# A Conformer block with its convolution moved into one attention loop over both batches

## The chip, the cores and the metric

The kernel runs on one core of a Trainium2 chip. The metric is the device time of one execution in microseconds (us); the median of the runs shown is compared.

## What is computed

A macaron Conformer block on x of shape (2, 4000, 512) in bf16, width D = 512, feed-forward width F = 2048, kernel width K = 3:

```python
h = _layernorm(x);  x1 = x + 0.5 * (_silu(h @ w_ff1_a) @ w_ff1_b)
h = _layernorm(x1)
q, k, v = h @ w_q, h @ w_k, h @ w_v
p = _softmax(einsum('btd,bsd->bts', q, k) * D ** -0.5)
x2 = x1 + einsum('bts,bsd->btd', p, v) @ w_o
h = _layernorm(x2) @ w_pw1
h = h[..., :D] * _sigmoid(h[..., D:])
hp = pad(h, one row of zeros before and after each batch)
dc = sum over i of hp[:, i:i + T, :] * dw[i]
dc = (dc - mean) / sqrt(var + 1e-5)      # mean and var over all 8000 rows
x3 = x2 + _silu(dc) @ w_pw2
x4 = x3 + 0.5 * (_silu(_layernorm(x3) @ w_ff2_a) @ w_ff2_b)
return _layernorm(x4)
```

The statistics of dc need every row of both batches before the first row of x3 can be formed.

## The kernel before

The 8000 rows are 16 chunks of 500 (eight per batch), each four tiles of 125 rows. x stays in SBUF for the whole kernel and is updated in place by `residual` (VectorE). Every matmul product is laid out so that TensorE streams 500 or 512 columns. There are eight PSUM banks: four "score" banks handed out in a ring by `sbank` (tile `s` in the profile), four "Y" banks (tile `y`) for sums that run over many steps.

The order of work is written out by hand. Each loop step emits its matmuls, then `hook` and `tick`; `after(n, fn)` puts `fn` n ticks ahead, `lags` holds the second half of earlier steps, and `pop` emits it. Each engine runs its instructions in the order emitted, waiting on semaphores that `Sync` derives from buffers read and written; a transfer's waits stand in the queue of the engine that issues it.

- `ln_job`: LayerNorm of a chunk: four `bn_stats` and aggregates on VectorE, a power on GpSimd, four normalisations (L492 on VectorE or, for the conv stage, L439 on ScalarE), and four DMA transposes issued on SyncE (L447) that give the feature-major copy `lnT` (or `hT` for keys).
- `ff_chunk`: for each of 16 slices of F, four matmuls, Silu on ScalarE, and four steps later the four matmuls of the second product into the Y banks.
- Keys: `wq wk` and `wv wo` are folded into `M` and `Wvo` at the start, so the normalised rows themselves are keys and values: `h` (row-major, 32 tiles of 128 with three rows of zeros set by `zero_keys`, L869) and `hT`. One batch's keys fill the region named `keys`.
- `attention(b)`: for eight query chunks, 32 key tiles each: four score matmuls, Exp on ScalarE, a running f32 sum on VectorE (L635), and four key tiles later the four value matmuls. `q_group` makes the next chunk's queries at key tiles 14 to 20. `finish_queries` copies the four Y banks out (ScalarE and VectorE, L661), splits the running sum in two bf16 halves (L665, L666), and puts `sums` two ticks and four `project` steps four to seven ticks later.
- `conv`: for 16 chunks and four feature blocks jj, the two halves of pw1 (eight matmuls), Sigmoid on ScalarE, the product on VectorE into `G` (L710), one-column halo copies on GpSimd, and one chunk later `depthwise`: three matmuls with diagonal tap matrices (`taps`), a copy to `dcv` on ScalarE and `bn_stats` on VectorE. `dcv` of all 16 chunks fills the `keys` region, free after attention.
- After the statistics: `swish` (ScalarE) and `pw2` (16 matmuls) of four chunks ahead, then FF2 over 16 chunks with `swish` and `pw2` of later chunks in its hook, and `out_job` for the last LayerNorm and the store.

`program` runs: FF1 of batch 0, attention of batch 0, FF1 of batch 1, attention of batch 1, conv, FF2. The weights of FF1 are loaded on ScalarE's queue at the start; FF2's first weights (`load_wa`) on SyncE's during the second attention, its second ones (`load_wb`) after conv. A second copy of the program, for scores too large for an unshifted exponential, is compiled behind a flag (`any_score`) and does not run on these inputs.

Of the kernel before, what the change touches and what calls it, by code (L numbers as in the profile page):

```python
# [13 lines left out]
TILE = 125  # L14
# [38 lines left out]
class Sync:  # L53
# [3 lines left out]
    def __init__(self, nc, n_dma_sems=40):  # L57
# [131 lines left out]
class Region:  # L189
# [13 lines left out]
    def buf(self, name, off, nbytes):  # L203

        assert off + nbytes <= self.nbytes, name
        b = Buf(name)
        for lo, hi, a in self.spans:
            if lo < off + nbytes and off < hi:
                b.alias.append(a)
                a.alias.append(b)  # L210
        self.spans.append((off, off + nbytes, b))
        return b


class Conformer:
    LN_SLOTS = 4
    NP = 8
    NG = 3
# [11 lines left out]
    def memory(self):  # L230
# [16 lines left out]
        self.dcv = [[A.view(t * 4096 + cc * 1024, CHUNK) for cc in range(DC)] for t in range(NCK)]  # L247
        self.b_dcv = [[A.buf("dcv", t * 4096 + cc * 1024, 1000) for cc in range(DC)]
# [11 lines left out]
        self.b_Wa = [Buf("Wa%d" % k) for k in range(self.NWA)]  # L260
# [46 lines left out]
        self.Wp1 = C.view(oM, DC * 2 * D).rearrange("p (c f) -> p c f", c=DC)  # L307
        self.b_Wp1 = C.buf("Wp1", oM, 8192)
# [4 lines left out]
        gof = [16384 + k * 4096 for k in range(self.NG)]  # L313
# [4 lines left out]
        o = 16384 + self.NG * 4096  # L318
        self.sig = [W.view(o + s * 1024, CHUNK) for s in range(2)]
        self.b_sig = [W.buf("sig", o + s * 1024, 1000) for s in range(2)]  # L320
        o += 2048
        self.bst = W.view(o, DC * NCK * 6, F32).rearrange("p (c t s) -> p c t s", c=DC, t=NCK)
        self.b_bst = [W.buf("bst", o + cc * NCK * 24, NCK * 24) for cc in range(DC)]
        self.dwd = [C.view(oACC + i * 256, 128) for i in range(DC * KW)]
        self.b_dwd = [C.buf("dwd", oACC + i * 256, 256) for i in range(DC * KW)]
# [6 lines left out]
        assert off[0] == 47104  # L332

# [55 lines left out]
        self.b_out = [Buf("out%d" % c) for c in range(NCK)]  # L389

# [50 lines left out]
    def load(self, dst, src, writes, eng="SP"):  # L441
        k = self.S.dsems[self.nxt("ld", 12)]
        return self.S.dma(eng, k, lambda e: e.dma_start(dst, src), writes=writes)

    def transpose(self, dst, src, reads, writes):
        k = self.S.dsems[12 + self.nxt("tr", 16)]
        return self.S.dma("SP", k, lambda e: e.dma_start_transpose(dst, src), reads=reads, writes=writes)  # L447

# [51 lines left out]
    def ln_job(self, c, at, kind, eng="DVE", gap=1):  # L500
# [3 lines left out]
        def tile(ti):  # L504
            if kind == "key":
                k = c % TCB
                tok, b_tok = self.h[k * TPC + ti], self.b_h[k * TPC + ti]
                feat, b_feat = self.hT[k][:, ti], self.b_hT[k][ti]
            else:
                tok, b_tok = self.ltm[ti], self.b_ltm[ti]  # L510
                feat, b_feat = self.lnT[c % 2][:, ti], self.b_lnT[c % 2][ti]
            self.ln_norm(c, sl, ti, tok[0:TILE, :], b_tok, eng)
            self.transpose(feat, tok, [b_tok], [b_feat])
# [98 lines left out]
    def attention(self, b, old, hook, done):  # L612
        S = self.S
        LAG = 4
        for qc in range(TCB):
            s = qc % 2
            if self.any_score:
                self.row_max(qc)
            for kt in range(TB):
# [19 lines left out]
                def values(kt=kt, p=p, qc=qc):  # L639
# [8 lines left out]
                if qc == 0 and kt < LAG:  # L648
                    self.pop({0: old // 2, 1: old - old // 2}.get(kt, 0))
                else:  # L650
# [43 lines left out]
    def conv(self, old, hook):  # L694
        S = self.S
        for t in range(NCK):
            gs, gp = t % self.NG, (t - 1) % self.NG
            for jj in range(DC):
                halves = []
                for cb in (DC + jj, jj):  # L700
                    ps, b_ps = self.sbank()
                    out = ps[:, 0:CHUNK].rearrange("p (t k) -> p t k", t=TPC)
                    for cc in range(DC):
                        self.mm(out, self.Wp1[:, cc, cb * 128:(cb + 1) * 128], self.lnT[t % 2][:, :, cc, 0:TILE],
                                cc == 0, cc == DC - 1, [self.b_Wp1] + self.b_lnT[t % 2], b_ps)
                    halves.append((ps, b_ps))
                (pb, b_pb), (pa, b_pa) = halves
                ss = self.nxt("sig", 2)
                self.act(self.sig[ss], pb[:, 0:CHUNK], AF.Sigmoid, [b_pb], [self.b_sig[ss]])
                S.op("DVE", lambda e, pa=pa, ss=ss, jj=jj, gs=gs: e.tensor_tensor(  # L710
                    out=self.G[gs][:, jj, 1:1 + CHUNK], in0=pa[:, 0:CHUNK], in1=self.sig[ss], op=ALU.mult),
                    reads=[b_pa, self.b_sig[ss]],
                    writes=[self.b_G[gs][jj], self.b_Gl[gs][jj], self.b_Gr[gs][jj]])
                self.halo(t, jj)
                if t >= 1:
                    self.lags.append(lambda t=t, jj=jj: self.depthwise(t - 1, jj))
                if t == NCK - 1:
                    self.lags.append(lambda t=t, jj=jj: self.depthwise(t, jj))
                if t == 0:
                    self.pop({0: old // 2, 1: old - old // 2}.get(jj, 0))  # L720
                elif t > 1 or jj > 1:
                    self.pop(1)
                hook(t, jj)
                self.tick()

    def halo(self, t, jj):

        S = self.S
        gs, gp = t % self.NG, (t - 1) % self.NG
# [11 lines left out]
    def depthwise(self, t, cc):  # L741
        S, gs = self.S, t % self.NG
# [20 lines left out]
    def taps(self):  # L763
# [6 lines left out]
        S.op("DVE", lambda e: e.tensor_copy(self.dwT, ps[:, 0:DC * KW].rearrange("p (c k) -> p c k", c=DC)),  # L770
             reads=[b_ps], writes=[self.b_dwT])
        for i in range(DC * KW):
            S.op("DVE", lambda e, i=i: e.tensor_scalar(
                self.dwd[i], self.ident, self.dwT[:, i // KW, i % KW:i % KW + 1], None, ALU.mult),
                reads=[self.b_ident, self.b_dwT], writes=[self.b_dwd[i]])
# [91 lines left out]
    def zero_keys(self):  # L867
        for k in range(TB):
# [3 lines left out]
    def program(self, any_score):  # L872
# [21 lines left out]
        self.zero_keys()  # L894
# [7 lines left out]
        def ff1(c, old):  # L902
            def hook(f):
                if f == 0 and c + 2 < NCK:
                    self.load_x(c + 2)
                if f == 1 and c + 1 < NCK and (c + 1) % TCB:
                    self.ln_job(c + 1, 1, "in")
                if c == 0 and f == 8:
                    weights()
                if c == NCK - 1 and f == 1:  # L910
                    pass

            self.ff_chunk(c, old, hook, lambda: self.ln_job(c, 5, "key"))

        def ff2_weights():
            for k in range(self.NWA):
# [118 lines left out]
```

## Time and profile before

| | us |
|---|---|
| median of 3 runs | 2277.57 (2275.61 to 2277.70) |
| profiled execution | 2278.08 |
| its span, first to last instruction | 2274.3 |

| engine | busy us | share |
|---|---|---|
| TensorE (PE), matmuls | 2131.4 | 94% |
| VectorE (DVE) | 989.3 | 43% |
| ScalarE (ACT) | 804.1 | 35% |
| GpSimd (POOL) | 122.0 | 5% |

The mean granted TensorE clock is 0.974. In the profile's lines the first numbers of a timeline row are its start and duration in us, "x" counts instructions merged in it, and "[t <-who]" is the engine's idle time just before it and what ended it. L435 is the helper through which every matmul goes, L439 that of every ScalarE instruction, L443 and L447 those of loads and transposes. SPq and ACTq are DMA issues in those engines' queues. Tile names are those of memory regions: `work`, `wff`, `keys`, `xt`.

### The profile page before, as it was taken

What the parts mean: (1) busy time and instruction counts of PE and PEld (TensorE: products, weight loads), DVE (VectorE), ACT (ScalarE), POOL (GpSimd) and SP (SyncE); (2) the same over time, 40 slices, a digit from 0 to 9 for tenths busy, and PEclk for the clock granted to TensorE, in tenths of its full rate; (3) what the DMA queues carried; (4) which work ended last, traced back from release to release, by engine and by line L of the source; (5) the groups of instructions that cost most, each with busy time, mean ns of one, the idle gap of its engine ahead of it and who ended that gap; (6) DMA issues with size and microseconds to landing.
All of it is one profiled execution on the core that took longest, in us unless ns stands there. A gap on an engine that the chain in (4) does not pass through costs nothing.

```text
span 2274.3 us, 24679 instructions
## 1 busy us (share of the span) xinstructions
PE 2131.4 (94%) x9828; PEld 1063.6 (47%) x9830; DVE 989.3 (43%) x2013; ACT 804.1 (35%) x1362; POOL 122.0 (5%) x283
## 2 busy tenths in 40 slices
PE   3999999999999999999999999977677999999996
PEld 1555544444444555544444444432233555555553
DVE  4333344444445344334444444554445543444432
ACT  1433333333333333333333333333445433333332
POOL 3000000000000000000000000011111000000000
PEclk9999999999999999999999999988778999999998
DMA  7122000000000022220000000011112111111110
GB/s 166 36 60 58 23 10 1 1 1 1 1 1 13 25 56 56 37 56 1 1 1 1 1 1 4 26 29 37 35 30 56 24 33 37 37 32 34 35 41 27
DMA packets 176144, 63.69 MB, mean 28 GB/s; under 512 B 146194, under 2 KB 175509, under 8 KB 176021
## 3 DMA queue, kind: packets, MB, share of 16 engines
q1 hardware_dynamic: 169620, 57.84, 11.4%
q10 hardware_dynamic: 6400, 4.20, 0.7%
q8 instruction: 79, 1.29, 0.2%
q14 instruction: 45, 0.36, 0.0%
HBM read 18.68 MB, written 8.19 MB: 12 GB/s over the span
## 4 chain that ended last, share of the span: by engine, by line
PE 87%; DVE 6%; ACT 3%; issue 2%; POOL 1%; DMA 1%; SPq 0%; POOLq 0%; DVEq 0%; ACTq 0%
PE s L435 49%; PE y L435 38%; ACT work L439 2%; DVE work L469 2%; POOL work L479 1%; DVE work L661 1%; DVE work L492 1%; DVE wff L749 1%; DVE work L666 0%; DMA xt<-in_x_dram 0%; DVE work L635 0%; ACT keys L439 0%; ACT wff L439 0%; DVE work L475 0%; DVE work L665 0%
## 5 line engine op out<-in xcount | busy, mean ns | idle before, releaser
L439 ACT ACTIVATE work<-s 128x500 bf16<-128x500 f32 (+1 forms) x1068 | 626.5, 587 | 1270.2 <-PE s L435 1265.1
L435 PE MATMUL y<-wff,work 128*125 128x512 bf16 (+1 forms) x2240 | 574.2, 384 | 0.0
L435 PE MATMUL s<-work,wff 128*128 128x500 bf16 x2048 | 511.2, 378 | 35.7 <-DMA work<-work 35.7
L635 DVE TENSOR_TENSOR work<-work 128x500 f32<-128x500 f32 x496 | 336.9, 679 | 474.1 <-ACT work L439 473.2
L435 PE MATMUL y<-work,keys 128*128 128x500 bf16 x2048 | 519.0, 374 | 2.0
L435 PE MATMUL s<-work,keys 128*128 128x500 bf16 x2048 | 517.4, 375 | 0.3
L435 PEld LDWEIGHTS y<-wff,work 128*125 128x125 bf16 (+1 forms) x2240 | 301.2, 134 | 204.2 <-issue 11.2
L435 PE MATMUL s<-work 128*128 128x500 bf16 (+3 forms) x1158 | 296.6, 393 | 87.6 <-ACT wff L439 64.1
L435 PEld LDWEIGHTS s<-work,wff 128*128 128x128 bf16 x2048 | 200.9, 98 | 258.0 <-issue 39.2
L435 PEld LDWEIGHTS y<-work,keys 128*128 128x128 bf16 x2048 | 198.1, 97 | 244.5 <-DVE work L661 15.3
L435 PEld LDWEIGHTS s<-work,keys 128*128 128x128 bf16 x2048 | 199.2, 98 | 229.0 <-DVE work L572 1.2
L530 DVE SCALAR_TENSOR_TENSOR xt<-y,xt 125x512 bf16<-125x512 f32 x128 | 79.5, 684 | 384.9 <-PE y L435 384.9
L435 PEld LDWEIGHTS s<-work 128*125 128x125 bf16 (+2 forms) x1158 | 137.9, 128 | 224.6 <-ACT wff L439 75.7
L469 DVE BATCH_NORM_STATS2 work<-xt 125x6 f32<-125x512 bf16 x320 | 200.3, 680 | 7.5 <-DMA xt<-in_x_dram 7.5
L479 POOL TENSOR_TENSOR work<-work 125x4 f32<-125x4 f32 x80 | 80.7, 1008 | 1928.5 <-DVE work L477 1928.5
L530 DVE SCALAR_TENSOR_TENSOR xt<-s,xt 125x512 bf16<-125x512 f32 x64 | 43.8, 691 | 132.5 <-PE s L435 132.5
L710 DVE TENSOR_TENSOR wff<-s,wff 128x500 bf16<-128x500 f32 x64 | 43.4, 677 | 113.4 <-ACT wff L439 77.4
L492 DVE TENSOR_SCALAR work<-xt,work 125x512 bf16<-125x512 bf16 x196 | 85.5, 482 | 11.0 <-POOL work L479 10.7
L439 ACT ACTIVATE work<-xt,work 125x512 bf16<-125x512 bf16 x60 | 43.9, 801 | 79.2 <-POOL work L486 79.2
L435 PE MATMUL s<-keys,work 128*128 128x500 bf16 x256 | 63.9, 376 | 0.0
L530 DVE SCALAR_TENSOR_TENSOR xt<-s,work,xt 125x512 bf16<-125x512 f32 x64 | 48.1, 751 | 29.3 <-PE s L435 29.3
L749 DVE BATCH_NORM_STATS2 wff<-keys 128x6 f32<-128x500 bf16 x64 | 43.2, 675 | 25.0 <-ACT keys L439 24.7
(46 smaller groups left out, 372.3 us busy)
## 6 DMA issues: line engine op xcount, KB each, us to landing
xt<-in_x_dram SPq DMA_DIRECT2D x15, 500.0 KB
out_dram<-work SPq DMA_DIRECT2D x15, 500.0 KB
work<-work SPq DMA_TRANSPOSE x192, 2.5
wff<-in_w_ff_a_dram ACTq DMA_DIRECT2D x8, 256.0 KB
wff<-in_w_ff_b_dram ACTq DMA_DIRECT2D x8, 256.0 KB
wff<-in_w_ff_a_dram SPq DMA_DIRECT2D x8, 256.0 KB
wff<-in_w_ff_b_dram SPq DMA_DIRECT2D x4, 512.0 KB
keys<-keys SPq DMA_TRANSPOSE x64, 2.4
```

Source lines behind the costliest of these rows:

```text
L435: self.S.op("PE", lambda e: e.matmul(out, lhsT, rhs, start=start, stop=stop), reads=reads, writes=[bank], inc=stop if inc is None else inc)
L439: return self.S.op("ACT", lambda e: e.activation(out, in_, func, **kw), reads=reads, writes=writes)
L469: self.S.op("DVE", lambda e: e.bn_stats(self.st[sl][:, ti, :], self.XT[g]), reads=[self.bx[g]], writes=[self.b_st[sl][ti]])
L479: S.op("POOL", lambda e: e.tensor_tensor(out=self.rs[sl], in0=self.va[sl], in1=self.neghalf[0:TILE, :], op=ALU.pow), reads=[self.b_va[sl], ...
L492: self.S.op("DVE", lambda e: e.tensor_scalar(out, self.XT[g], self.mv[sl][:, ti, 0:1], self.rs[sl][:, ti:ti + 1], ALU.subtract, ALU.mult), ...
L530: self.S.op("DVE", lambda e: e.scalar_tensor_tensor(out=self.XT[g], in0=ps, scalar=scalar, in1=self.XT[g], op0=ALU.mult, op1=ALU.add), rea ...
L635: S.op("DVE", lambda e, p=p: e.tensor_tensor(out=self.acc[s], in0=self.acc[s], in1=self.P[p], op=ALU.add), reads=[self.b_P[p], self.b_acc[ ...
L661: S.op("DVE", lambda e, dc=dc: e.tensor_copy(self.OT[:, dc, :], self.Yb[dc][:, 0:CHUNK]), reads=[self.b_Y[dc]], writes=[self.b_OT[dc]])
L710: S.op("DVE", lambda e, pa=pa, ss=ss, jj=jj, gs=gs: e.tensor_tensor(out=self.G[gs][:, jj, 1:1 + CHUNK], in0=pa[:, 0:CHUNK], in1=self.sig[s ...
L749: S.op("DVE", lambda e: e.bn_stats(self.bst[:, cc, t, :], self.dcv[t][cc]), reads=[self.b_dcv[t][cc]], writes=[self.b_bst[cc]])
```

## The change

FF1 runs over all 16 chunks first. Batch 0's keys go to `h` and `hT` as before; batch 1's normalised rows (`"key2"`) go through a staging tile `h2` to an HBM tensor `keys2`. One attention loop then runs over all 16 query chunks g; `second_keys` loads and transposes batch 1's key tiles from HBM as batch 0's tiles are used up, from key tile 6 of g = 7 to key tile 5 of g = 8. The LayerNorm of a finished query chunk starts with its last `project`, its normalisations on VectorE. Its pw1 work is issued in four `pair`s: at key tiles 22 and 27 of the next query chunk and 1 and 6 of the one after. A pair is `conv_b` (four matmuls, Tanh) and one tick later `conv_a` (four matmuls, the gate from sigmoid(b) = (1 + tanh(b / 2)) / 2, with the factor of a half put into the taps). Chunks 0 to 12 take their taps on VectorE (`taps_beside`: three operations, the middle results in f32, then `bn_stats`) and store the result to the HBM tensor `dcvd`; `fetch_conv` brings it back into `dcv` during the last query chunk and after it. Chunks 13 to 15 keep `depthwise` on TensorE, with pw1 of chunks 14 and 15 behind the loop. Wp1 now lies over FF1's first weights, so all FF2 weights are loaded after the last pw1, on ScalarE's queue: five pieces before the last two `depthwise`, the rest behind them and behind a Silu of one element. `zero_keys` is split over the FF1 chunks 0 to 7; the taps are prepared during FF1.

```diff
+        self.Wp1 = W.view(0, DC * 2 * D).rearrange("p (c f) -> p c f", c=DC)
+        self.b_Wp1 = W.buf("Wp1", 0, 8192)
...
+        self.stage = [W.view(8192 + cc * 1024, CHUNK) for cc in range(DC)]
+        self.b_stage = [W.buf("stage", 8192 + cc * 1024, 1000) for cc in range(DC)]
+        self.tmp = W.view(12288, CHUNK, F32)
+        self.b_tmp = W.buf("tmp", 12288, 2000)
+        self.bst = W.view(14848, DC * NCK * 6, F32).rearrange("p (c t s) -> p c t s", c=DC, t=NCK)
+        self.b_bst = [W.buf("bst", 14848 + cc * NCK * 24, NCK * 24) for cc in range(DC)]
+        gof = [16384, 20480]
...
+        self.h2 = [C.view(oQ1 + j * 1024, D) for j in range(TPC)]
+        self.b_h2 = [C.buf("h2", oQ1 + j * 1024, 1024) for j in range(TPC)]
...
+        self.keys2 = nc.dram_tensor("keys2", [TB * 128, D], BF16, kind="Internal").ap()
...
+        self.dcvd = nc.dram_tensor("dcvd", [self.NBESIDE, 128, DC * CHUNK], BF16, kind="Internal").ap()
...
+            if kind == "key2":
+                self.ln_norm(c, sl, ti, self.h2[ti][0:TILE, :], self.b_h2[ti], eng)
+                if ti == TPC - 1:
+                    k = c % TCB
+                    dst = self.keys2[k * 512:(k + 1) * 512, :].rearrange("(t p) d -> p t d", p=128)
+                    self.store(dst, self.h2c, self.b_h2, [self.b_keys2[k]])
+                return
...
-        for qc in range(TCB):
+        for g in range(NCK):
+            b, qc = divmod(g, TCB)
...
-                if qc + 1 < TCB and kt in (14, 16, 18, 20):
-                    self.q_group(b, qc + 1, (kt - 14) // 2)
-                hook(qc, kt)
+                if g + 1 < NCK and kt in (14, 16, 18, 20) and not (self.any_score and g + 1 == TCB):
+                    self.q_group((g + 1) // TCB, (g + 1) % TCB, (kt - 14) // 2)
+                if not self.any_score:
+                    if g == TCB - 1 and kt >= 6:
+                        self.second_keys(kt - 6)
+                    if g == TCB and kt < 6:
+                        self.second_keys(TB - 6 + kt)
+                hook(g, kt)
                 self.tick()
+    def second_keys(self, kt):
+        kc, kj = divmod(kt, TPC)
+        src = self.keys2[kt * 128:(kt + 1) * 128, :]
+        self.load(self.h[kt], src, [self.b_h[kt]], reads=[self.b_keys2[kc]])
+        self.transpose(self.hT[kc][:, kj], src, [self.b_keys2[kc]], [self.b_hT[kc][kj]])
...
-        self.after(2, sums)
+        last = b * TCB + qc == NCK - 1
+        self.after(1 if last else 2, sums)
         for ti in range(TPC):
-            self.after(4 + ti, lambda ti=ti: project(ti))
...
+            self.after((2 if last else 4) + ti, lambda ti=ti: project(ti))
...
+    def conv_b(self, t, jj):
+        ps, b_ps = self.pw1(t, DC + jj)
+        k = jj % 2
+        self.act(self.th[k], ps[:, 0:CHUNK], AF.Tanh, [b_ps], [self.b_th[k]], scale=0.5)
+    def conv_a(self, t, jj):
+        ps, b_ps = self.pw1(t, jj)
+        k, gs = jj % 2, t % 2
+        self.S.op("DVE", lambda e: e.scalar_tensor_tensor(
+            out=self.G[gs][:, jj, 1:1 + CHUNK], in0=self.th[k], scalar=1.0, in1=ps[:, 0:CHUNK],
+            op0=ALU.add, op1=ALU.mult),
+            reads=[b_ps, self.b_th[k]],
+            writes=[self.b_G[gs][jj], self.b_Gl[gs][jj], self.b_Gr[gs][jj]])
+        self.halo(t, jj)
+    def pw1(self, t, cb):
+        s = 1 if t == NCK - 1 else 0
+        ps, b_ps = self.sbank()
+        out = ps[:, 0:CHUNK].rearrange("p (t k) -> p t k", t=TPC)
+        for cc in range(DC):
+            self.mm(out, self.Wp1[:, cc, cb * 128:(cb + 1) * 128], self.lnT[s][:, :, cc, 0:TILE],
+                    cc == 0, cc == DC - 1, [self.b_Wp1] + self.b_lnT[s], b_ps)
+        return ps, b_ps
+    def taps_beside(self, t, cc):
+        S, g = self.S, self.G[t % 2][:, cc, :]
+        rd = [self.b_G[t % 2][cc], self.b_Gl[t % 2][cc], self.b_Gr[t % 2][cc], self.b_dwT]
+        w = [self.dwT[:, cc, k:k + 1] for k in range(KW)]
+        tmp, b_tmp = self.tmp, self.b_tmp
+        S.op("DVE", lambda e: e.tensor_scalar(tmp, g[:, 0:CHUNK], w[0], None, ALU.mult), reads=rd, writes=[b_tmp])
+        S.op("DVE", lambda e: e.scalar_tensor_tensor(
+            out=tmp, in0=g[:, 1:1 + CHUNK], scalar=w[1], in1=tmp, op0=ALU.mult, op1=ALU.add),
+            reads=rd + [b_tmp], writes=[b_tmp])
+        def rest():
+            S.op("DVE", lambda e: e.scalar_tensor_tensor(
+                out=self.stage[cc], in0=g[:, 2:2 + CHUNK], scalar=w[2], in1=tmp, op0=ALU.mult, op1=ALU.add),
+                reads=rd + [b_tmp], writes=[self.b_stage[cc]])
+            S.op("DVE", lambda e: e.bn_stats(self.bst[:, cc, t, :], self.stage[cc]),
+                 reads=[self.b_stage[cc]], writes=[self.b_bst[cc]])
+            self.store(self.dcvd[t][:, cc * CHUNK:(cc + 1) * CHUNK], self.stage[cc],
+                       [self.b_stage[cc]], [self.b_dcvd[t][cc]])
+        self.after(1, rest)
+    def fetch_conv(self, t):
+        self.load(self.dcv4[t], self.dcvd[t].rearrange("p (c k) -> p c k", c=DC), self.b_dcv[t],
+                  reads=self.b_dcvd[t])
...
-        self.zero_keys()
...
-                if f == 1 and c + 1 < NCK and (c + 1) % TCB:
+                if f == 1 and c + 1 < NCK:
                     self.ln_job(c + 1, 1, "in")
+                if c < TCB and f == 6:
+                    self.zero_keys(c)
                 if c == 0 and f == 8:
                     weights()
...
+                if c == 1 and f == 1:
+                    self.load(self.dwr, i["dw"], [self.b_dwr])
+                    self.after(6, self.taps)
+                if c == TCB - 1 and f < TPC:
+                    self.S.op("POOL", lambda e: e.memset(self.h2[f], 0.0), writes=[self.b_h2[f]])
+            self.ff_chunk(c, old, hook, lambda: self.ln_job(c, 5, "key" if c < TCB else "key2"))
...
+        for c in range(NCK):
+            ff1(c, old)
             old = len(self.lags)
...
+        for dc in range(DC):
+            self.q_group(0, 0, dc)
+        def pair(t, jj):
+            self.conv_b(t, jj)
+            self.after(1, lambda: self.conv_a(t, jj))
+            if t > 0:
+                self.after(3, lambda: self.taps_beside(t - 1, jj))
+        tail = NCK - 2
+        def att_hook(g, kt):
+            if g == 0 and kt == 8:
+                self.load(self.Wp1, i["w_pw1"].rearrange("(c p) f -> p c f", p=128), [self.b_Wp1])
+            if 0 <= g - 1 < tail and kt in (22, 27):
+                pair(g - 1, (22, 27).index(kt))
+            if 0 <= g - 2 < tail and kt in (1, 6):
+                pair(g - 2, 2 + (1, 6).index(kt))
+            if g == NCK - 1:
+                if 8 <= kt < 20 and not any_score:
+                    self.tap_matrix(kt - 8)
+                if kt >= 8 and kt % 4 == 0:
+                    for t in (kt // 4 - 2, TCB + kt // 4 - 2):
+                        if t < self.NBESIDE:
+                            self.fetch_conv(t)
+        self.attention(old, att_hook, lambda c: self.ln_job(
+            c, 1, "in", gap=1 if c < NCK - 1 else 0, slot=1 if c == NCK - 1 else 0))
+        if any_score:
+            for k in range(DC * KW):
+                self.tap_matrix(k)
+        steps = []
+        for jj in range(DC):
+            steps += [lambda jj=jj: self.conv_b(tail, jj), lambda jj=jj: self.conv_a(tail, jj)]
+        self.pop(3)
+        steps.pop(0)()
+        steps.pop(0)()
+        self.pop(1)
+        self.tick()
+        steps.pop(0)()
+        for _ in range(5):
+            self.tick()
+        while steps:
+            steps.pop(0)()
+            self.tick()
+        for cc in range(DC):
+            self.depthwise(tail - 1, cc)
+            self.tick()
+        for t in range(6, TCB):
+            self.fetch_conv(t)
+        while self.later:
+            self.tick()
+        self.load(self.Wp2, i["w_pw2"].rearrange("(c p) f -> p c f", p=128), [self.b_Wp2])
+        for jj in range(DC):
+            self.conv_b(tail + 1, jj)
+            if jj:
+                self.depthwise(tail, jj - 1)
+            self.conv_a(tail + 1, jj)
+            if jj:
+                self.depthwise(tail + 1, jj - 1)
+        clear = (14848 - 12288) // (F // self.NWA * 2)
+        for k in range(clear):
+            self.load_wa(i["w_ff2_a"], k, "ACT")
+        self.depthwise(tail, DC - 1)
+        self.depthwise(tail + 1, DC - 1)
+        self.act(self.nr1, self.onef, AF.Silu, [self.b_onef], [self.b_nr1])
+        for k in range(clear, self.NWA):
+            self.load_wa(i["w_ff2_a"], k, "ACT")
         for k in range(4):
-            self.load_wb(i["w_ff2_b"], 4 * k, 4 * k + 4)
+            self.load_wb(i["w_ff2_b"], 4 * k, 4 * k + 4, "ACT")
```

More of the change, by code (lines that the diff above doesn't have):

```diff
@@ L203, in buf, with bufs @@
     def buf(self, name, off, nbytes):
-        assert off + nbytes <= self.nbytes, name
+        return self.bufs(name, [(off, nbytes)])
+    def bufs(self, name, pieces):
         b = Buf(name)
[L207 to L211, printed above, removed]
+        for off, nbytes in pieces:
+            assert off + nbytes <= self.nbytes, name
+            for lo, hi, a in self.spans:
+                if lo < off + nbytes and off < hi and a not in b.alias:
+                    b.alias.append(a)
+                    a.alias.append(b)
+        self.spans += [(off, off + nbytes, b) for off, nbytes in pieces]
         return b
@@ L940, in conv_hook @@
-        def conv_hook(t, jj):
-            if t == 0 and jj == 2:
-                self.load(self.dwr, i["dw"], [self.b_dwr])
-                self.after(2, self.taps)
-            if t == 4 and jj == 0:
-                self.load(self.Wp2, i["w_pw2"].rearrange("(c p) f -> p c f", p=128), [self.b_Wp2])
-            if jj == 0 and t + 1 < NCK:
-                self.ln_job(t + 1, 0, "in", "ACT", gap=0)
-        self.conv(old, conv_hook)
-        self.drain()
+                if c == 1 and f == 1:
+                    self.load(self.dwr, i["dw"], [self.b_dwr])
+                    self.after(6, self.taps)
```

129 lines of the change are left out of this document (43 added, 86 removed).

## Prediction

> **What bounds the kernel now.** I read the page's busy shares and slices first, then busy time by stage, then what TensorE waited for, then the timeline at the three places where it idles.
>
> ```profile
> span 2274.3 us, 24679 instructions
> PE   3999999999999999999999999977677999999996
> PEclk9999999999999999999999999988778999999998
> 274.00:765.00 491.00, 485.88 (x2316) 227.17 (x2314) 226.51 (x360) 166.37 (x285) 2.01 (x2) 1.00 0.02 4
> 1484.00:1758.00 274.00, 197.66 (x728) 80.75 (x726) 132.12 (x287) 116.43 (x194) 40.05 (x173) 0.81 0.17 39
> PE s L435 <- ACT wff L439: 64.1, 14, 4.7
> PE s L435 <- DMA work<-work: 35.7, 1, 35.7
> PE s L435 <- DVE work L666: 7.8, 16, 0.5
> ```
>
> Lines 2 and 3 are tenths in 40 slices; the two rows with a colon give, for one stage, its length and the busy time of PE, PEld, DVE, ACT, POOL, then granted clock, DMA share and GB/s. TensorE is the bound everywhere but in two places: the first slice and the conv stage. The first attention keeps it busy 485.88 of 491 us at clock 1.00, DVE and ACT under half. The conv stage has 197.66 of 274 us at clock 0.81, and those busy microseconds are stretched. The last rows are TensorE's waits (total, times, longest): 14 waits on ACT in the conv stage, one start wait of 35.7 us.
>
> One step of the conv stage shows why:
>
> ```profile
> 1518.06 1.86 PE L435 MATMUL s<-work 128*128 128x500 bf16 x8
> 1519.48 2.46 DVE L469 BATCH_NORM_STATS2 work<-xt 125x6 f32<-125x512 bf16 x4
> 1524.11 2.93 ACT L439 ACTIVATE work<-xt,work 125x512 bf16<-125x512 bf16 x4 [5.26 <-POOL work L486]
> 1526.94 0.56 ACT L439 ACTIVATE wff<-s 128x500 bf16<-128x500 f32 x1
> 1527.56 3.52 PE L435 MATMUL s<-work 128*128 128x500 bf16 x8 [4.67 <-ACT wff L439]
> ```
>
> The next chunk's LayerNorm (stats, POOL, four norms on ACT) sits in ACT's queue ahead of a sigmoid, a score bank stays full, TensorE waits 4.67 us, and its next eight matmuls take 3.52 instead of 1.86 us. This happens once a chunk.
>
> **The change part by part.** Only TensorE's line and what holds it count.
>
> *1. Conv stage out, pw1 woven in.*
>
> ```profile
> 1479.09 1.86 PE L435 MATMUL s<-work 128*128 128x500 bf16 x8
> 1482.48 1.86 PE L435 MATMUL s<-work 128*128 128x500 bf16 x8
> 1484.18 1.85 PE L435 MATMUL y<-work,keys 128*128 128x500 bf16 x8
> 1756.74 9.80 PE L435 MATMUL s<-work 128*125 128x512 bf16 x32 [6.55 <-ACT work L439]
> 263.23 3.41 PE s L435 x16
> ```
>
> The last attention values end at 1484.18 + 1.85 = 1486.0; the two pw1 steps already woven in (16 matmuls) are 16 x 0.213 = 3.4 us, where 0.213 is 3.41 / 16 from the last row, four q groups of the same shape. So attention alone ends near 1482.5, and the first pw2 matmul starts at 1756.74: the old stage costs 274.2 us, its tail of sums, projection and final statistics included. In the new loop stand chunks 0 to 13 (14 x 32 = 448 matmuls) and the first pair of chunk 14 (8): 456 x 0.213 = 97.1 us. The depthwise matmuls of chunks 0 to 12, 13 x 12, are gone from TensorE at no cost if DVE carries the taps.
>
> DVE's load: 226.51 us over eight query chunks is 28.3 each. Added per chunk are four LayerNorm norms (they were on ACT), four stats, four gating products, and 16 tap operations, 28 in all.
>
> ```profile
> L635 DVE TENSOR_TENSOR work<-work 128x500 f32<-128x500 f32 x496 | 336.9, 679 | 474.1 <-ACT work L439 473.2
> 102.18 2.55 PE s L435 x12
> 129.59 2.55 PE s L435 x12
> 984.31 3.41 PE s L435 x16
> ```
>
> At 0.679 us each (row L635, the same width in f32) that is 19 us, DVE 47 per chunk. The two PE rows lie one FF chunk apart, 27.41 us; the q groups at 263.23 and 984.31 lie 721.1 apart, so attention of one batch is 721.1 - 8 x 27.41 = 501.8, 62.7 per query chunk, and with 32 woven matmuls 69.5. DVE is at two thirds: it hides. Tanh replaces sigmoid (0.59 us either way by shape) in ACT's free half. The woven groups take score banks exactly as q groups and projections do, and TensorE's waits list no ACT or DVE release for those, only 0.5 us a chunk for the sums. So I take 0 for friction; below nothing is excluded, as no work goes; above I put 0.25 us a pair, 56 x 0.25 = 14, half of that 0.5 us wait.
>
> *2. FF1 of both batches in one run.* The same 16 chunks at 27.41; keys of batch 1 go to HBM from DVE and SP, off the path: 0. Reading them back adds 32 loads and 32 transposes to SP, a pair per key tile.
>
> ```profile
> 1487.13 5.12 SPq L447 DMA_TRANSPOSE work<-work  x4
> 43.13 3.10 SPq L447 DMA_TRANSPOSE keys<-in_w_k_dram  x1
> ```
>
> A transpose holds SP 1.28 us (5.12 / 4); a key tile of the new loop lasts 69.5 / 32 = 2.17, so SP keeps up, with the LayerNorm transposes and tap stores of the same chunk queued behind it: 0. The upper end is the transpose out of HBM, 3.10 us though four times larger; see rivals.
>
> *3. Zeroing of the keys moved into FF1.*
>
> ```profile
> 13.86 14.99 POOL L869 MEMSET keys<- 128x512 bf16 x32
> 13.94 16.01 DVE L492 TENSOR_SCALAR work<-xt,work 125x512 bf16<-125x512 bf16 x4 [1.15 <-POOL work L479]
> L492 DVE TENSOR_SCALAR work<-xt,work x196: 394/408/15051, 13.9 to 2264.0; 125x512 bf16<-125x512 bf16 x196
> 29.02 5.22 SPq L447 DMA_TRANSPOSE work<-work  x4
> 35.70 7.07 PE L435 MATMUL s<-work,wff 128*128 128x500 bf16 x20 [35.70 <-DMA work<-work]
> 15.00:20.00 5.00, 0.00 (x0) 0.00 (x0) 5.00 (x1) 1.28 (x1) 5.00 (x12) 1.00 0.99 264
> 25.00:30.00 5.00, 0.00 (x0) 0.00 (x0) 5.00 (x5) 0.00 (x0) 3.84 (x9) 1.00 0.00 0
> ```
>
> One of the first four norms took 15.05 us instead of 0.41, as long as the burst of memsets beside it. Transposes follow the norm, TensorE follows the transposes 1.46 us after their issue ends (29.02 + 5.22 to 35.70). Without the burst the norms end near 15.6, transposes issue 14.4 to 19.7, TensorE starts at 21.2 at best. The weight loads fill the DMA engines then (0.99) and are done by 25 us (share 0.00), so the worst is 25 + 1.5 = 26.5. I take 23, nearer the free case because only the last of four transposes must land: gain 12.7, ends 9.2 and 14.5. Next in line are the weights, of which the first chunk needs the first pieces only. The four memsets now issued in FF1 chunks 0 to 7 (2.1 us) can hold a norm that has most of 27 us to spare: 0.
>
> The Trainium skill, SBUF — State Buffer, section Who interferes with whom, says that a GpSimd operation and a VectorE operation in a two-port mode lock each other out for one whole instruction. By that a norm would lose one memset (0.53 us), not 28 in a row; the row shows the whole burst. By the rule alone the move would gain next to nothing and the sum would be 12 us higher; the row decides.
>
> *4. The new tail, from the last values (t0) to the first pw2 matmul.*
>
> ```profile
> 1490.32 1.25 DVE L661 CAST work<-y 128x500 bf16<-128x500 f32 x2
> 1491.93 0.68 DVE L666 TENSOR_TENSOR work<-work 128x500 bf16<-128x500 f32 x1
> 1763.74 2.46 DVE L469 BATCH_NORM_STATS2 work<-xt 125x6 f32<-125x512 bf16 x4
> 1768.25 21.76 SPq L447 DMA_TRANSPOSE work<-work  x8
> 1745.59 4.60 PE L435 MATMUL y<-wff,work 128*128 128x500 bf16 x21
> L443 ACTq DMA_DIRECT2D wff<-in_w_ff_a_dram x8: 428/487/1054, 0.8 to 14.6; - x8
> L443 ACTq DMA_DIRECT2D wff<-in_w_ff_b_dram x8: 530/1020/2571, 1.2 to 15.1; - x8
> ```
>
> Row by row: copies and sums' input 2.3 us (1490.32 to 1492.61), sums 0.7, projection 16 x 0.215 = 3.4, residual 1: t0 + 7.4. LayerNorm of chunk 15: 4.5 us from stats to first transpose (1763.74 to 1768.25), four issues 5.1, landing 1.5: t0 + 18.5. Beside it lie the rest of chunk 14 and depthwise 13 (36 matmuls, 7.7 us). Then chunk 15 with depthwise 14 and 15: 56 x 0.213 = 11.9, plus 3 for one slow restart (3.52 - 1.86) and halo waits: t0 + 33.4. The old run from the last depthwise (1745.59 + 4.60) to pw2 is 6.5. New on ACT's queue are twelve weight loads: five ahead of the last two copies (5 x 0.49 = 2.4), seven ahead of the first swish (3 x 0.49 + 4 x 1.02 = 5.5, of which about 3 stand where ACT idled): +5. Sum 45; at least 30, the TensorE work plus 6.5; at most 55, with issues at their slow ends and two more restarts. The 4.2 MB of FF2 weights then load beside the pw2 groups instead of attention; at the start 4.2 MB landed by 25 us and FF2 begins some 30 us after the first issue: 0, and up to 3 if they delay the first FF2 transposes (inside the 55).
>
> **Sum.** 274.2 - 97.1 - 45 = 132.1 saved in conv, 12.7 at the start: 144.8. The profiled execution took 2278.08 (median of the runs 2277.57), so 2133. Low end: 2278 - (274.2 - 97.1 - 30) - 14.5 = 2116.
>
> **Rivals.** *A, slower: waits at the woven pairs.* Each pair takes two of the four score banks, one released only through DVE's in-order queue, now two thirds full. Place: key tiles 1, 6, 22, 27. It decides from 144.8 / 56 = 2.6 us a pair. One wait like the conv stage's (4.67, then 1.66 of slow restart) per pair gives 56 x 6.3 = 354: 2487. Against it: q groups in the same banks cause none, and three banks' work, over 4 us, lies between a pair and the reuse of its bank.
>
> *B, table reloads.* If Tanh and Exp cannot stay loaded together, 56 pairs cost two loads each.
>
> ```profile
> L439 ACT ACT_TABLE_LOAD x6 | 7.7, 1283 | 17.5 <-DMA wff<-in_w_ff_b_dram 16.3 <-PE s L435 1.1
> ```
>
> 56 x 2 x 1.283 = 144 us on ACT: hidden by the four-tile lag 2133, all on the path 2277, half 2205. The six loads are one per stage; no row shows Tanh. The Trainium skill, ScalarE: Activation LUTs, section Table sets: the hidden batching unit, lists tanh in the set of exp, so it speaks for no reload; it also lists tanh in sigmoid's set.
>
> *C, the start stays.* If loads, not memsets, set it, TensorE starts at 35.7: 2146.
>
> *D, SP falls behind* with HBM transposes at 3.10 us plus a load: about 1.4 us late per key tile, which pushes back the LayerNorm transposes of two chunks by 10 each: 2153.
>
> **How the numbers follow.** Forecast 0.68, A 0.04, B 0.06, C 0.10, D 0.12. Range 2116 to 2165: it holds the forecast with its bounds, C and D, and 14 of pair friction with the long tail; A and most of B are left out. 0.2% (4.6 us) is about what a measurement here can tell from no change: faster 0.95 (B's far end excepted), same 0.01, slower 0.04.
>
> **What would show it.** Right: TensorE at 9 in all slices but the first and one near the tail, granted clock 1.00 there; three table loads; first matmul at 21 to 27 us; query chunks 69 to 70 us apart from the second on; DVE's share of the loop near two thirds; t0 to pw2 at 45. Wrong: query chunks over 72 us, TensorE waits on DVE or ACT at the pairs, more than 100 table loads, SP's transposes bunched at query chunks 7 and 8, or ACT's weight loads stretching the tail past 55.

## The result and the profile after

| | before | after |
|---|---|---|
| median, us | 2277.64 | 2136.32 |
| profiled execution, us | 2278.08 | 2136.0 |
| its span, us | 2274.3 | 2132.2 |
| TensorE busy | 94% | 97% |
| granted clock | 0.974 | 0.992 |

The ratio is 0.9378, 95% interval [0.9362, 0.9394]; the forecast was 2133 in a range of 2116 to 2165. Executions of the kernel before lie near 2270 or near 2277 us, so ratios taken on different chips differ by some 0.3%, and one run below, of 2784 us at a granted clock of 0.752, is left out of its median. The page of the changed kernel, TensorE's slices and granted clock:

```profile
span 2132.2 us, 24365 instructions
PE   4999999999999999999999999999987999999996
PEclk9999999999999999999999999999999999999998
```

The dip of five slices is down to two. Where the time went is read from both traces, cut at the same events: first matmul, first q group (twice before), last attention values (before: their end at 1486.0 less 3.4 us for the two pw1 steps that already stood among them), first pw2 matmul, end. Columns: stretch and length; busy time of PE, PEld, DVE, ACT, POOL; granted clock, DMA share, GB/s. Before, busy time by stage:

```profile
0.00:35.70 35.70, 0.00 (x0) 0.03 (x1) 24.44 (x30) 1.28 (x1) 18.30 (x46) 1.00 0.60 161
35.70:263.23 227.53, 227.43 (x1049) 122.95 (x1052) 72.23 (x200) 82.14 (x144) 13.11 (x13) 1.00 0.28 60
263.23:984.31 721.08, 715.58 (x3394) 352.75 (x3392) 311.24 (x584) 245.14 (x418) 16.12 (x16) 1.00 0.08 17
984.31:1482.50 498.19, 493.61 (x2353) 230.92 (x2352) 231.40 (x368) 169.52 (x289) 2.12 (x3) 1.00 0.03 9
1482.50:1756.74 274.24, 197.90 (x733) 81.11 (x732) 133.62 (x289) 115.17 (x192) 40.05 (x173) 0.82 0.17 37
1756.74:2274.30 517.56, 496.93 (x2304) 275.85 (x2304) 216.39 (x544) 190.88 (x319) 32.26 (x32) 0.98 0.14 34
```

After, the same view:

```profile
0.00:28.79 28.79, 0.01 (x1) 0.04 (x2) 8.66 (x27) 1.28 (x1) 3.54 (x15) 1.00 0.95 203
28.79:476.19 447.40, 447.40 (x2079) 242.92 (x2080) 174.24 (x444) 157.31 (x272) 45.95 (x65) 1.00 0.23 56
476.19:1571.86 1095.67, 1086.85 (x5176) 507.98 (x5174) 666.61 (x1168) 369.01 (x633) 36.46 (x124) 1.00 0.11 28
1571.86:1614.57 42.71, 28.07 (x117) 12.49 (x117) 24.69 (x48) 14.10 (x25) 4.59 (x22) 0.85 0.39 110
1614.57:2132.20 517.63, 496.57 (x2304) 275.31 (x2304) 216.29 (x544) 190.97 (x319) 32.32 (x32) 0.98 0.15 36
```

The start fell by 6.9. FF1 of both batches is 447.4 against 227.5 + 8 x 27.41 = 446.8. The attention of both batches was 721.1 + 498.2 - 219.3 = 1000.0 and is 1095.7 with the woven pw1: plus 95.7. The stretch from the last values to pw2 fell from 274.2 to 42.7: minus 231.5. FF2 is unchanged. Together minus 142.1, the difference of the spans.

In the chain of work, two rows at the same place of neighbouring query chunks:

```profile
617.04 3.41 PE s L453 x16
686.46 3.41 PE s L453 x16
```

They are 69.42 us apart. TensorE's waits in the changed kernel (sum, count, longest):

```profile
PE s L453 <- DMA work<-work: 28.8, 1, 28.8
PE s L453 <- DVE work L716: 7.9, 16, 0.5
PE s L453 <- ACT work L457: 7.9, 1, 7.9
PE s L453 <- DVE wff L755: 3.4, 1, 3.4
```

The 14 waits on ACT are gone, and no pair inside the loop waits: the one wait on ScalarE and the one on the gate (L755) are in the tail.

### The profile page after: what moved, and what is told of

Read it like the earlier page. It is cut to its first block, busy times and chain, and to the rows that moved or that the text cites. A ratio compares the mean times of both kernels' runs of the same rounds, so it can differ in the third digit from the quotient of the medians.

```text
span 2132.2 us, 24365 instructions
## 1 busy us (share of the span) xinstructions
PE 2058.9 (97%) x9674; PEld 1038.7 (49%) x9674; DVE 1090.5 (51%) x2229; ACT 732.7 (34%) x1248; POOL 122.9 (6%) x257
## 3 DMA queue, kind: packets, MB, share of 16 engines
q8 instruction: 78, 1.28, 0.3%
## 4 chain that ended last, share of the span: by engine, by line
PE 93%; DVE 3%; issue 1%; DMA 1%; ACT 0%; SPq 0%; POOL 0%; ACTq 0%; POOLq 0%; DVEq 0%
PE s L453 53%; PE y L453 39%; DVE work L711 1%; DVE work L716 1%; DVE work L673 0%; DMA xt<-in_x_dram 0%; ACT work L457 0%; DVE work L491 0%; SPq L465 0%; DMA work<-work 0%; DVE work L715 0%; DVE work L514 0%; POOL work L501 0%; DVE xt L560 0%; ACTq L461 0%
## 5 line engine op out<-in xcount | busy, mean ns | idle before, releaser
L453 PE MATMUL s<-work,wff 128*128 128x500 bf16 x2560 | 634.3, 378 | 32.2 <-DMA work<-work 28.8
L453 PE MATMUL y<-wff,work 128*125 128x512 bf16 x2048 | 514.8, 379 | 0.0
L453 PEld LDWEIGHTS s<-work,wff 128*128 128x128 bf16 x2560 | 251.1, 98 | 313.3 <-issue 33.7
L453 PEld LDWEIGHTS y<-wff,work 128*125 128x125 bf16 x2048 | 279.6, 137 | 176.4
L453 PE MATMUL s<-work 128*125 128x512 bf16 (+2 forms) x646 | 144.8, 347 | 20.8 <-DVE work L716 7.9
L514 DVE TENSOR_SCALAR work<-xt,work 125x512 bf16<-125x512 bf16 x288 | 116.0, 449 | 20.1 <-POOL work L501 20.1
L453 PEld LDWEIGHTS s<-work 128*125 128x125 bf16 (+1 forms) x646 | 81.1, 139 | 72.1 <-issue 10.8
L755 DVE SCALAR_TENSOR_TENSOR wff<-wff,s 128x500 bf16<-128x500 f32 x64 | 43.2, 676 | 63.7 <-PE s L453 63.7
L457 ACT ACTIVATE wff<-s 128x500 f32<-128x500 f32 x64 | 37.6, 587 | 81.3 <-PE s L453 76.8
L457 ACT ACTIVATE work<-keys,work 128x500 bf16<-128x500 bf16 x64 | 49.6, 794 | 5.9 <-DMA wff<-in_w_ff_a_dram 4.0
```

The lines of the kernel that those rows point to most:

```text
L453: self.S.op("PE", lambda e: e.matmul(out, lhsT, rhs, start=start, stop=stop), reads=reads, writes=[bank], inc=stop if inc is None else inc)
L457: return self.S.op("ACT", lambda e: e.activation(out, in_, func, **kw), reads=reads, writes=writes)
L514: self.S.op("DVE", lambda e: e.tensor_scalar(out, self.XT[g], self.mv[sl][:, ti, 0:1], self.rs[sl][:, ti:ti + 1], ALU.subtract, ALU.mult), ...
L755: self.S.op("DVE", lambda e: e.scalar_tensor_tensor(out=self.G[gs][:, jj, 1:1 + CHUNK], in0=self.th[k], scalar=1.0, in1=ps[:, 0:CHUNK], op ...
```

## The experiments

The theory: the gain is TensorE's time in the conv stage, refilled inside a loop in which every other engine has room; VectorE's taps and SyncE's transfers cost nothing; the start's gain is the memset burst, capped by weight loads.

**Only the memsets split**, on the kernel before:

```diff
-        self.zero_keys()
+                if c < TCB and f == 6:
+                    self.zero_keys(c)
```

> The kernel before with one edit: the 32 memsets of the key tiles are issued four at a time in the FF1 chunks of batch 0 instead of in one burst at the start. Theory: the burst held one normalisation for 15.05 us, and what is left once it is gone is the contention of the weight loads, so the first matmul moves from 35.7 to about 28.8 us, as in the changed kernel, and the whole time falls by 6.9 us. Rival 1 (the prediction's sum): the first matmul at 23, minus 12.7 us. Rival 2: the loads alone set the start, first matmul stays at 35.7, 0 us.

The median was 2270.4 against 2275.8 of the kernel before on that chip, ratio 0.998 [0.997, 0.999]. Its timeline at the start:

```profile
14.15 1.38 DVE L492 TENSOR_SCALAR work<-xt,work 125x512 bf16<-125x512 bf16 x4 [1.15 <-POOL work L479]
14.59 10.33 SPq L447 DMA_TRANSPOSE work<-work  x4
28.61 6.84 PE L435 MATMUL s<-work,wff 128*128 128x500 bf16 x20 [28.61 <-DMA work<-work]
```

The norms take 1.38 us instead of 16.01: the burst was what held them. The first matmul moves by 7.1 us, as in the changed kernel, so this part is the whole of the start's gain. The transposes then take 10.33 us to issue where they took 5.22 alone. In the whole time the gain is less sure: the twelve runs take 2267.9 to 2271.6 us, but six of the seventeen of the kernel before took 2269.4 to 2271.2 as well. None of those was traced, so it stays open whether the burst holds a norm in every execution.

**Ten weight loads behind the transposes**, on the changed kernel:

```diff
-        for k in range(self.NWA):
+        for k in range(3):
             self.load_wa(i["w_ff1_a"], k, "ACT")
...
+        for k in range(3, self.NWA):
+            self.load_wa(i["w_ff1_a"], k)
+            self.load_wb(i["w_ff1_b"], 2 * k, 2 * k + 2)
```

> The changed kernel with one edit: of FF1's sixteen weight loads only the first six (1.5 of 4.2 MB) are issued ahead of the first chunk's DMA transposes, the other ten follow the transposes on SyncE's queue. Theory: in the changed kernel the transposes were ready to issue at 14.5 us but took 10.2 us to issue and 4 more to land because the weight loads kept the DMA engines busy; with the loads behind them they issue in 5.2 us and the first matmul comes at 21 to 22 us instead of 28.8, minus 7 us on the whole, if the late weights still arrive ahead of TensorE. Rival 1: the four transposes are slow for another reason (first use), first matmul stays near 28.8, 0 us. Rival 2: the late weights starve the first FF1 chunk, and what is gained up to 22 us is lost by 60 us.

2128.3 us, ratio to before 0.936 [0.9343, 0.9377]. Its timeline:

```profile
13.79 5.23 SPq L465 DMA_TRANSPOSE work<-work  x4
20.46 6.44 PE L453 MATMUL s<-work,wff 128*128 128x500 bf16 x20 [20.46 <-DMA work<-work]
```

With fewer loads in flight the issue is back at 5.23 us, TensorE starts at 20.46, and nothing is lost later (its first q group is 9.2 us earlier than in the changed kernel). The loads were what held the start next, once the burst was gone.

**Sigmoid for Tanh**, on the changed kernel:

```diff
-        self.act(..., AF.Tanh, ..., scale=0.5)
+        self.act(..., AF.Sigmoid, ...)
-            op0=ALU.add, op1=ALU.mult),
+            op0=ALU.mult, op1=ALU.mult),
```

> The changed kernel with Sigmoid in place of Tanh in the gate (the product and the factor of the taps adapted). It prices the prediction's rival B: 56 pairs inside the loop would each reload the activation table twice, 112 loads of 1.283 us, 144 us of ScalarE. If ScalarE's free time and the four-tile lag hide them: 0 to 5 us more than the changed kernel, query chunks still 69.4 us apart. If they stand on TensorE's path: up to 144 us more, query chunks up to 79.7 us apart. I expect something between and nearer to hidden: a pair holds the score bank of the next key tile for about 3.2 us, and three other banks give TensorE some 2.5 us, so under 1 us a pair, 0 to 50 us in all.

2135.9 us, ratio 0.9386 [0.9368, 0.9404], as the changed kernel. ScalarE's group of table loads (count, busy time, mean ns) in the changed kernel and then here, and its timeline here at one pair:

```profile
L457 ACT ACT_TABLE_LOAD x3 | 3.8, 1283 | 16.8 <-DMA wff<-in_w_ff_b_dram 16.8
L457 ACT ACT_TABLE_LOAD x116 | 148.8, 1283 | 18.7 <-DMA wff<-in_w_ff_b_dram 16.6
```

```profile
652.22 1.28 ACT L457 ACT_TABLE_LOAD   x1
653.51 0.59 ACT L457 ACTIVATE wff<-s 128x500 f32<-128x500 f32 x1
654.12 1.28 ACT L457 ACT_TABLE_LOAD   x1
655.41 0.59 ACT L457 ACTIVATE work<-s 128x500 bf16<-128x500 f32 x1
656.69 0.59 ACT L457 ACTIVATE work<-s 128x500 bf16<-128x500 f32 x1 [0.70 <-PE s L453]
658.38 0.59 ACT L457 ACTIVATE work<-s 128x500 bf16<-128x500 f32 x1 [1.10 <-PE s L453]
```

113 more loads and 145 us more of ScalarE cost nothing, and query chunks stay 69.42 us apart: a pair makes the exponential late, and two key tiles on ScalarE waits 1.10 us for TensorE again, as in the changed kernel. Rival B was both absent (the changed kernel has three loads) and, on this path, free.

**The taps back on TensorE**, on the changed kernel:

```diff
     def taps_beside(self, t, cc):
+        ps, b_ps = self.sbank()
+        for k in range(KW):
+            self.mm(ps[:, 0:CHUNK], self.dwd[cc * KW + k], self.G[gs][:, cc, k:k + CHUNK], ...)
+        self.act(self.stage[cc], ps[:, 0:CHUNK], AF.Copy, ...)
```

> The changed kernel with the taps of chunks 0 to 12 back on TensorE inside the loop: three matmuls with the diagonal tap matrices into a score bank, a copy on ScalarE, the statistics on VectorE; the tap matrices are made in the first query chunk. Theory: VectorE's taps are wholly hidden and TensorE is the bound, so 156 matmuls at 0.213 us come back, 33.2 us on the whole, 2.56 us per query chunk (69.4 to 72.0), while VectorE's busy time falls by some 100 us. Rival 1: taps on VectorE cost the loop something by its in-order queue; then the change is smaller than 33. Rival 2: a fifth taker of score banks adds waits, larger than 33.

2160.0 us, ratio 0.9501 [0.9478, 0.9523]: slower than the changed kernel, but by 24 us in the spans, not 33, while VectorE's busy time falls by 87 us. Query chunks are 71.32 apart, plus 1.90: nine matmuls at 0.211, where twelve were added. The missing three are, by their place, those at key tile 4. TensorE's own waits do not show it; the weight loads' (PEld) do (sum, count, longest). First the changed kernel, then this one:

```profile
PEld y L453 <- DVE work L711: 15.6, 30, 0.6
PEld s L453 <- DVE work L716: 9.3, 16, 0.6
```

```profile
PEld y L453 <- DVE work L711: 2.1, 4, 0.6
```

At each change of chunk the first value matmuls wait for VectorE's copies of the Y banks, twice about 0.5 us, and the sums for the split of the running sum. The matmuls at key tile 4 fell into that hole. The kernel before has it too (15.3 us over 28 waits for the Y copies).

**One pair moved into the hole**, on the changed kernel:

```diff
-            if 0 <= g - 2 < tail and kt in (1, 6):
-                pair(g - 2, 2 + (1, 6).index(kt))
+            if 0 <= g - 2 < tail and kt in (3, 6):
+                pair(g - 2, 2 + (3, 6).index(kt))
```

> The changed kernel with one pw1 pair per chunk moved from key tile 1 to key tile 3 of the query chunk, between the last value matmuls of the chunk before and the first of the new one. With the taps on TensorE, three of twelve depthwise matmuls per chunk cost nothing (1.90 us a chunk instead of 2.53), and the weight loads' waits for the Y-bank copies fell from 15.6 to 2.1 us: theory, TensorE waits about 0.5 us per chunk for the Y copies and 0.5 more for the split of the running sum, and matmuls put there fill it. Then query chunks go from 69.4 to 68.4 to 68.9 us, minus 7 to 14 us in all. Rival: the copies and the split simply come later by the gate's own work on ScalarE and VectorE, 0 us.

2118.5 us, ratio 0.931 [0.9296, 0.9324]. One chunk by stage view, in the changed kernel and then here:

```profile
686.46:755.88 69.42, 68.85 (x329) 32.21 (x328) 43.72 (x77) 23.27 (x40) 2.59 (x9) 1.00 0.06 16
```

```profile
682.73:750.92 68.19, 68.19 (x329) 32.28 (x328) 43.53 (x78) 23.27 (x40) 3.41 (x9) 1.00 0.06 16
```

The weight loads' wait here:

```profile
PEld y L453 <- DVE work L711: 1.1, 2, 0.6
```

The same 329 matmuls in 1.23 us less per chunk, TensorE busy all of it: both Y-copy waits and the sums' wait are filled, some 17 us over the chunks that have such a pair, above the 7 to 14 expected, which counted one Y copy and not two.

**Taps three times**, on the changed kernel (each tap operation issued three times):

```diff
+        for _ in range(3):
             S.op("DVE", lambda e: e.tensor_scalar(tmp, g[:, 0:CHUNK], w[0], ...
```

> The changed kernel with each of the three tap operations on VectorE issued three times, with the same result: 312 more operations, some 201 us of VectorE more, its share of a query chunk from 43.7 of 69.4 us to about 59. Theory: VectorE is off TensorE's path with room left, query chunks stay at 69.4 us, 0 to 5 us in all. Rival: the in-order queue releases score banks and Y banks late once bursts of taps (some 4 us) stand ahead of a gate product or a Y copy; then query chunks grow, by up to 15 us each if nothing is hidden, 201 us in all.

2140.6 us, ratio 0.9404 [0.939, 0.9419]. A stretch of its loop by engine, and then TensorE's wait on VectorE (sum, count, longest):

```profile
1036.00:1106.00 70.00, 69.07 (x330) 32.13 (x328) 58.25 (x101) 23.33 (x41) 3.82 (x12) 1.00 0.11 28
```

```profile
PE s L453 <- DVE xt L560: 6.9, 14, 3.4
```

VectorE is at 58 of 70 us. In the traces the loop from first q group to the last sixteen value matmuls grew by 5.9 us (1089.9 to 1095.8), 3% of what was added. The new wait is on projection residuals queued behind taps: 3.6 us over 13 waits inside the loop, none above 0.4 (the longest of the row, 3.4, is in the tail, where the changed kernel has it too). The rival's mechanism exists, and at three times the load it is worth some 0.45 us a chunk; at the changed kernel's load it does not show.

**Norms of the conv stage on VectorE**, on the kernel before:

```diff
-                self.ln_job(t + 1, 0, "in", "ACT", gap=0)
+                self.ln_job(t + 1, 0, "in", "DVE", gap=0)
```

> The kernel before with the LayerNorm norms of its conv stage on VectorE instead of ScalarE. Reading A (the prediction's account of the conv stage): four norms of 0.80 us in ScalarE's queue ahead of the sigmoid are what keeps TensorE waiting 4.67 us a chunk and slow after it; without them the stage loses most of 14 x 6.3 = 88 us. Reading B: the stage's pitch of 17.05 us a chunk is set by the whole chain of the next chunk's LayerNorm (stats, power, norms, transposes), which starts only when the chunk before begins; then only the shorter norms and the two GpSimd steps left out count, about 2 us a chunk, 30 us, and TensorE waits for something else.

2270.5 us, ratio 0.9964 [0.9948, 0.9979]. Four of its ten runs take 2260 to 2262 us at a granted clock of 0.984 to 0.986, six 2270 to 2273 at 0.976 to 0.978; the trace is of one of 2261.8. What TensorE waited for (sum, count, longest):

```profile
PE s L435 <- DMA work<-work: 65.5, 10, 35.4
PE s L435 <- DVE wff L710: 21.6, 13, 1.8
```

The waits on ScalarE are gone, and 51.7 us of others stand there: the transposes of the next chunk (65.5 less the start's 35.4) and the gate on VectorE. From the start of the last value matmuls to the first pw2 matmul it is 255.8 us against 272.6, 16.7 less, with a granted clock of 0.90 there against 0.81. Reading A, which the prediction gave, falls: most of 88 us would have gone. Reading B fits better, as TensorE now meets the end of the next LayerNorm, its landed transposes, nine times; but its 30 us were too many, the waits on the gate are not part of it, and no run shortens the LayerNorm itself, so what sets the stage's pitch is not shown in full.

**FF2's loads on SyncE**, on the changed kernel (`"ACT"` taken off the twelve loads):

> The changed kernel with the twelve loads of FF2's weights in the tail issued on SyncE's queue instead of ScalarE's. Theory: their issue held ScalarE 2.07 us ahead of the last two copies and 2.3 us ahead of the first swish, so the time from the last depthwise matmul to the first pw2 matmul falls by 4.4 us, and so does the whole. Rival: the loads only move the wait, because SyncE then issues the first FF2 chunk's transposes later, or ScalarE waits for the statistics anyway: 0 to 2 us.

2130.0 us, ratio 0.936 [0.9347, 0.9373]. The timeline of ScalarE and of TensorE's first pw2 matmul in the changed kernel's tail, and then here:

```profile
1604.40 2.61 ACTq L461 DMA_DIRECT2D wff<-in_w_ff_a_dram  x5
1607.06 0.59 ACT L457 ACTIVATE keys<-y 128x500 bf16<-128x500 f32 x1 [2.07 <-DMA wff<-in_w_ff_a_dram]
1613.62 5.67 ACT L457 ACTIVATE work<-keys,work 128x500 bf16<-128x500 bf16 x8 [3.99 <-DMA wff<-in_w_ff_a_dram]
1614.57 9.45 PE L453 MATMUL s<-work 128*125 128x512 bf16 x32 [7.92 <-ACT work L457]
```

```profile
1606.26 3.26 SPq L461 DMA_DIRECT2D wff<-in_w_ff_b_dram  x4
1607.04 5.66 ACT L457 ACTIVATE work<-keys,work 128x500 bf16<-128x500 bf16 x8 [1.63 <-DVE work L830]
1607.98 6.29 PE L453 MATMUL s<-work 128*125 128x512 bf16 x17 [4.71 <-ACT work L457]
```

The first swish now waits for the statistics (L830) and not for load issues. TensorE's wait from the last depthwise matmul to pw2 falls from 7.92 to 4.71 us: minus 3.2, between the theory's 4.4 and the rival's 0 to 2. From the last sixteen value matmuls to pw2 it is 43.6 us against 48.5, but the other 1.7 us of that are not the loads': in the second trace of the changed kernel, below, that stretch is 46.6.

**Four edits together, and the changed kernel on the same chip.** The late FF1 weights, the FF2 loads on SyncE and the moved pair as above, and in the tail the second pair of chunk 14 ahead of the sums:

```diff
         self.pop(1)
+        steps.pop(0)()
+        steps.pop(0)()
         self.tick()
-        steps.pop(0)()
```

> The changed kernel with four edits together: ten of FF1's sixteen weight loads behind the first transposes, FF2's weight loads on SyncE, the pair of key tile 1 at key tile 3, and in the tail the second pair of chunk 14 ahead of the sums of chunk 15. If the parts add: first matmul at 20.5 us instead of 28.8 (minus 8.3), query chunks at 68.20 instead of 69.42 (minus 17), the tail 4.8 shorter by the loads and up to 2 by the order, 2136 minus 32, 2104 us. Rival: the tail's parts overlap (TensorE then waits for the LayerNorm of chunk 15 all the same), 2106 to 2108.

> The changed kernel as it is, on the same chip as the version with four edits, so that the two can be compared: 2133 to 2137 us, query chunks 69.42 us apart.

2106.7 us against 2134.7 for the changed kernel, ratios to before 0.9273 [0.9254, 0.9291] and 0.9395 [0.9377, 0.9414]: 28 us, 1.3%, faster than the change and the fastest here. Within the rival's 2106 to 2108: in the tail TensorE still waits 3.2 us for chunk 15's transposes, and from the last sixteen value matmuls to pw2 it is 44.4 us, 46.6 in the changed kernel on that chip, 43.6 with the loads alone moved. So the reordering brought nothing.

## Why the prediction was right, step by step

The account rests on two traces cut at the same events and on runs that change one part each. No run puts the woven pw1 back into a stage of its own; what the weaving as a whole is worth is read from the two traces.

*Conv out, pw1 in.* Forecast 274.2 out, 97.1 woven in, query chunks of 69.5: the trace has 95.7 and 69.42. Both the price per matmul and the zero for friction held: VectorE came to 43.7 us a chunk (47 forecast), no pair in the loop waits, and with VectorE at 58 us the loop grew by only 5.9. That the taps really leave TensorE, and what they are worth there, the taps on TensorE show: 24 us of the gain.

*Reading of the conv stage.* "The next chunk's LayerNorm sits in ACT's queue ahead of a sigmoid" was a correct row and a wrong cause: with the norms off ScalarE the stage lost 16.7 of its 272.6 us. The sum did not rest on it, as it counted the stage out as a whole.

*FF1 in one run, keys from HBM.* Zero forecast, 0.6 us found. The 32 key transposes held SyncE 1.19 to 1.20 us each almost throughout, near the 1.28 of the same shape from SBUF, not the 3.10 of rival D.

*The start.* This term failed: 12.7 forecast, 9.2 as its low end, 6.9 measured. The step was "landing": I let the transposes issue at their undisturbed 1.28 us each and placed contention only in the last landing, which I bounded by 25 us, the end of the weight loads, plus 1.5.

```profile
14.54 10.19 SPq L465 DMA_TRANSPOSE work<-work  x4
28.58 1.93 POOL L942 MEMSET keys<- 128x512 bf16 x4
28.74 1.90 DVE L514 TENSOR_SCALAR work<-xt,work 125x512 bf16<-125x512 bf16 x1 [1.21 <-POOL work L501]
```

Under the weight loads the issue itself took 10.19 us, and the landing after it 4.1 (24.73 to 28.79); with ten of the loads behind the transposes these are 5.23 and 1.4. The last rows are the first four memsets at their new place: a norm is again held for the whole group, 1.90 us. The Trainium skill, SBUF — State Buffer, section Who interferes with whom, gives the lock as lasting one instruction, which would be 0.53 us; the kind of contention agrees, the length does not, and the split run decides for the burst.

*The tail.* 45 forecast, 42.7 found. To the last depthwise matmul 33.4 was put and 34.8 found, from there to pw2 11.5 (6.5 and 5 for the loads) against 7.9; the twelve load issues on ScalarE cost 3.2 where 5 was put.

*Sum.* 144.8 forecast, 142.1 measured: the start 5.8 short, loop and tail 3.7 better, FF1 0.6 longer. That the misses nearly cancel is luck; that each is small beside 231.5 us out and 95.7 in is not. Rival A: no such wait. B: three table loads; the Trainium skill, ScalarE: Activation LUTs, section Table sets: the hidden batching unit, puts tanh into the set of exp, and the trace agrees. C: the split run refutes it. D: no wait on a transfer inside the loop.

## What to carry to other kernels

Price a stage that leaves the bound engine as a whole, between two events of that engine, and what comes back by a matmul of the same shape in a full stretch; that needs no account of the stage's inner waits. Look at the weight loads' waits as well as the matmuls': TensorE's row showed 0.5 us at each chunk change, the hole was 1.2, and work moved into it cost nothing here. At a start, a transfer's issue time is not a constant (5.2 or 10.2 us for the same four transposes here): put the loads that the first step doesn't need behind its transposes.

## What was not expected of the hardware

- Issue of a DMA transpose stretches under other loads: 1.3 us each with the DMA engines free, 2.5 while the 4.2 MB of weights were being loaded.
- 113 table loads among exponentials cost nothing in time here, and in the rows shown a load follows and precedes its neighbours within 0.03 us.
- One VectorE normalisation lasts as long as a whole group of back-to-back GpSimd memsets beside it, where it takes 0.41 us alone: 15.05 us for the rest of 32, 1.90 for four.
